# A fused attention and two-MoE kernel: the first token group's x prepared during the last pair of heads, the upper part of decoded weights written by ScalarE, and x items spread over each group

## The chip, the cores and the metric

The kernel runs on one core of a Trainium2 chip. The metric is the device time of one execution in microseconds (us); less is better. The engines of the core run side by side, each with its own instructions in program order: PE (TensorE, the matmuls), ACT (ScalarE), DVE (VectorE), POOL (GpSimd) and SP (SyncE, which here does little but issue DMAs). An instruction waits for semaphores that other engines or DMAs raise, and whatever stands behind it on its own engine waits with it.

## The reference, cut to what matters

```python
def _attn_ref(q, k, v):                       # 4 batches, 8 heads, 1152 positions, 64 per head
    q_pool = q.reshape(B, H, S // 2, 2, D).mean(axis=3)
    scores = np.matmul(q_pool, k.transpose(0, 1, 3, 2)) / np.sqrt(D)
    attn = np.exp(scores - scores.max(-1, keepdims=True))
    return np.matmul(attn / (attn.sum(-1, keepdims=True) + 1e-09), v)

def _moe_ref(x, w_in, w_out):                 # 2304 tokens, 512 -> 2048 -> 512
    h = x @ w_in
    g = np.where(h >= 1, h, np.where(h <= -1, 0.0, (h + 1) ** 2 / 4))
    return g @ w_out                          # then a second MoE: 8 experts, each token to one

reference: x = _moe2_ref(_moe_ref(concat_heads(_attn_ref(q, k, v)), w_in, w_out), ...)
```

The weights of the first MoE are handed in as float64; the kernel decodes them bit by bit.

## The kernel before

**Stages.** Attention runs first, then the dense MoE (called Moe1 here), then the one with experts. All products are done in split precision: a value is kept as an upper part in fp32r (`hi`) and the remainder (`lo = x - hi`), and products of parts are added.

**Attention.** 16 pairs of heads, 9 steps to a pair, 144 steps, numbered s, and 8 steps more to drain. The loop is `Attention.run`, its order is the order of the program. Step s issues the scores of tile s on PE into one PSUM buffer (`scores`), their row minimum and copy `e` on DVE, the transposes of tile s-2 on PE (`probs_t`), their upper part `pth` on ACT and the rest `ptl` on DVE, the exponential of tile s on ACT, and 8 of the matmuls with v (`av`) on PE. Results of `av` are copied to `avs` by ACT and sent to DRAM (`av_b`, `av_t`) by SP; sums of rows go to DRAM as `rs_b`. Raw q, k, v lie in a pool `a_prep`; POOL splits them for the next pair. The last pair is n = 15, steps 135 to 143.

**From attention to Moe1.** The first 640 tokens (group 0 of four) need x in SBUF, transposed. Three pieces of it come from DRAM for each of four row blocks: one part of the sums of products into `xth` and the reciprocals of the sums into `xtl` (`x_raw`, 32 DMAs in all, issued by SP), and the other part into staging tiles `rows` and `row` (`x_load`, 5 DMAs). Five items follow, one for each `parts` entry (`x_item`): two POOL operations (`x = (hi + x) * r`), and later `ev`: `xth` by an ACT copy and `xtl` by a DVE subtraction. Before the change `x_load` is issued at s = 135 (line 1428, in `aside`), the `a_prep` pool is given back at s = 141 and `x_raw` issued there (`tail`, called at line 380), and the items run from s = 144 on, in the drain. In SP's program order `x_load` comes first, then the DMAs of the sums and results of pair 14, then `x_raw`. Raw weights of Moe1 for j = 3 are loaded at s = 147.

**Moe1.** Four groups of tokens, 16 steps j each; step j takes 128 of the 2048 hidden columns. PE does `h` of step j in two halves of 320 tokens, 12 matmuls each (`h_mm`, two PSUM buffers), then the 15 matmuls of `y` of step j-1 (`y_mm`). Between them ACT and DVE make g of h (`h_act`): Relu and Square on ACT, one DVE operation that also sets the PSUM buffer of h free, the upper part `gh` on ACT, the rest `gl` on POOL (group 0) or DVE. During group 0 the weights for j = 3 to 15 are decoded: each has two halves, and each half is three pieces, `first`, `second` and `third`, one DVE operation each; `third` also makes the upper part `wh` and the rest `wl`, both on POOL. A piece is issued at each `fill()`: two in each half of a step and one at its end, five to a step. The x of the next group is made meanwhile: `x_raw` at j = 1, 3, 5, 7, `x_load` from j = 8, the items one after the other from j = 9.

Of the kernel before, what the change touches and what calls it, by code (L numbers as in the profile page):

```python
# [8 lines left out]
F32 = mybir.dt.float32  # L9
# [37 lines left out]
EARLY = 3  # L47
# [27 lines left out]
class Attention:  # L75
# [11 lines left out]
    def open(self, ctx):  # L87
        tc, nc = self.tc, self.nc

        def pool(name, bufs, **kw):  # L90
            return ctx.enter_context(tc.tile_pool(name=name, bufs=bufs, **kw))

        self.prep = tc.alloc_tile_pool(name="a_prep", bufs=1, side="right")
        self.ktp = pool("a_kt", 2)
        self.sp = pool("a_s", 3)
        self.sm = pool("a_sm", 3)
        one = pool("a_one", 1)
        self.ps_s = pool("a_ps_s", 1, space=PSUM)
        self.ps_a = pool("a_ps_a", 1, space=PSUM)
        self.ps_b = pool("a_ps_b", 1, space=PSUM)  # L100
        self.ps_v = pool("a_ps_v", 2, space=PSUM)
        self.pth = one.tile([128, 9, RING], F32R, name="pth")
        self.ptl = one.tile([128, 9, RING], F32R, name="ptl")
        self.vh = one.tile([128, 18, 128], F32R, name="vh")
        self.avs = one.tile([128, 2 * NQ], F32, name="avs")

        self.qts = [one.tile([128, 2, QW], F32R, name=f"qt{i}") for i in range(2)]

        self.bd = [one.tile([128, 2, 128], F32R, name=f"bd{i}") for i in range(2)]
        self.kk = one.tile([128, 2, S], F32R, name="kk")  # L110
        self.r = one.tile([128, 32], F32, name="r")
        self.nc.vector.memset(self.r, 1.0)
# [29 lines left out]
    def load_v(self, n):  # L142
        b, hp = divmod(n, 4)
        d = self.st[n]
        d["vr"] = self.prep.tile([128, 18, 64], F32, name="vr")
        self.nc.sync.dma_start(
            out=d["vr"].rearrange("p (h c) d -> p h c d", h=2),
            in_=self.v[b, 2 * hp:2 * hp + 2].rearrange("h (p c) d -> p h c d", p=128),
        )
# [171 lines left out]
    def run(self, aside, tail):  # L321
# [7 lines left out]
        g = collections.deque()  # L329
# [10 lines left out]
        for s in range(nt + 8):  # L340
# [36 lines left out]
            for _ in range(8 if s < nt else 16):  # L377
                if self.avq:
                    self.avq.popleft()()
            if s == nt - 3:  # L380
                self.prep.release()
                g.extend(tail())
            if self.post and self.post[0][0] < s:
                self.post.popleft()[1]()
            if s >= nt and g:
                for f in g.popleft():
                    f()
            aside(s)
# [8 lines left out]
class Weights:  # L397
# [38 lines left out]
    def decode(self, j):  # L436
# [7 lines left out]
        for i in range(2):  # L444
# [11 lines left out]
            def third(i=i, box=box):  # L456
                nc.vector.scalar_tensor_tensor(out=box["w"], in0=raw[j, i][:, :, 0], scalar=29, in1=box["w"],
                                               op0=ALU.logical_shift_right, op1=ALU.bitwise_or)
                w = box["w"].bitcast(F32)
                hi_part(nc.gpsimd, hi[:, i], w, nc)  # L460
                nc.gpsimd.tensor_sub(out=lo[:, i], in0=w, in1=hi[:, i].bitcast(F32))

            out += [first, second, third]
# [3 lines left out]
class Moe1:  # L467
# [151 lines left out]
    def run(self, route, xt2, moe2):  # L619
# [4 lines left out]
        for k in range(len(steps) + 1):  # L624
            self.flush()
            if k < len(steps):
# [3 lines left out]
                if j == 0 and g + 1 < ng:  # L630
# [12 lines left out]
                            load(i + 2)  # L643
                        return f
                    nxt = [lambda i=i, item=item: item(i) for i in range(m)]
                if g + 1 < ng and j in (1, 3, 5, 7):
                    self.x_raw(g + 1, [slice(j // 2, j // 2 + 1)])
                if g + 1 < ng and j == 8:
                    load(0)
                    load(1)  # L650
                if g + 1 < ng and j == 9:
                    self.xprep.extend(nxt)
                if (g, j) == (2, 10):
                    turn = route.turn(self)
                if (g, j) == (2, 12):
# [716 lines left out]
def tile_kernel(tc, q, k, v, w_in, w_out, emb, tau, w1, w2, out):  # L1372
    nc = tc.nc
    with ExitStack() as ctx:
# [19 lines left out]
        with ExitStack() as actx:  # L1394
# [14 lines left out]
            def aside(s):  # L1409
# [16 lines left out]
                if s == last:  # L1426
                    for i in range(5):
                        m1.x_load(0, i, ws.rows(i, 5))
                if s == last + 12:
                    ws.load(EARLY)  # L1430

            def tail():
# [72 lines left out]
```

## Time and profile before

| what | us |
|---|---|
| runs (3): median, lowest, highest | 1203.81, 1201.74, 1203.91 |
| the profiled execution | 1205.57 |
| its span, first to last instruction | 1203.8 |
| PE busy in the span | 1149.5 (95%) |
| DVE, ACT, POOL busy | 883.3 (73%), 740.3 (61%), 600.7 (50%) |
| TensorE's granted clock, mean | 0.983 |

The span is the time from the first to the last instruction of the profiled execution; 1.8 us more lie around it. Busy shares are means over stages: attention ends at about 481 us, group 0 of Moe1 lasts from there to about 622 us, Moe1 as a whole to about 920 us. A wait is read as the idle time of an engine ahead of an instruction and what ended it. The granted clock is given as a share of full speed, 2.4 GHz; its lower level is 0.5, 1.2 GHz.

### The profile page before, as it was taken

To read this page: it belongs to the slowest core of one execution; us is meant where nothing else is said; L and a number is where in the kernel's file an instruction comes from. 1 tells how busy PE (TensorE), PEld (TensorE's weight loads), DVE (VectorE), ACT (ScalarE), POOL (GpSimd) and SP (SyncE) were. 2 spreads that over 40 slices of the span, in tenths; PEclk is the share of its full clock that TensorE was granted. 3 is DMA by queue.
4 is the path that set the end of the run, shared out by engine and by line. 5 is a ranking of instruction groups with operands and counts; after the bars stand their busy time and mean duration, and the time that the engine had idled before them with its cause. 6 is when DMAs were issued, how large, how long until landed. Compare 5 with 4: busy or idle time off the path is not lost. (4 is left out here: it accounts for less than half of the span.)

```text
span 1203.8 us, 21165 instructions
## 1 busy us (share of the span) xinstructions
PE 1149.5 (95%) x7315; PEld 1068.2 (89%) x7315; DVE 883.3 (73%) x1593; ACT 740.3 (61%) x1451; POOL 600.7 (50%) x523
## 2 busy tenths in 40 slices
PE   7999999999999999799789999999999899999995
PEld 7999999999999999688679889988989798888794
DVE  6888988999999998698745664664444767576663
ACT  5888888878788787343335444444445466576663
POOL 7998988777888883699930230013020311122121
PEclk9999999999999999999899999999999899999998
DMA  7787777785868753564332212111240111376533
GB/s 187 179 184 179 165 186 171 171 209 126 205 162 205 173 137 103 158 194 147 101 106 65 66 45 76 56 34 31 97 159 27 40 51 38 116 256 191 177 106 110
DMA packets 87189, 156.14 MB, mean 130 GB/s; under 512 B 26871, under 2 KB 44279, under 8 KB 87056
## 3 DMA queue, kind: packets, MB, share of 16 engines
q1 hardware_dynamic: 82352, 142.34, 44.2%
q0 software_dynamic: 4336, 11.58, 2.9%
q8 instruction: 67, 1.10, 0.4%
q10 hardware_dynamic: 368, 0.59, 0.2%
q14 instruction: 66, 0.54, 0.2%
HBM read 145.84 MB, written 20.08 MB: 138 GB/s over the span
## 5 line engine op out<-in xcount | busy, mean ns | idle before, releaser
L235 DVE TENSOR_SCALAR_CACHE_REDUCE e<-sc 128x1152 f32<-128x1152 f32 x144 | 194.7, 1352 | 25.0 <-PE sc L231 23.8
L242 ACT ACTIVATE e<-e,nm 128x1152 f32<-128x1152 f32 x144 | 183.7, 1276 | 4.4 <-DVE e L235 4.4
L231 PE MATMUL sc<-kT,qt 128*128 128x384 f32 x780 | 159.8, 340 | 9.2 <-DVE e L235 7.5
L269 ACT CAST pth<-pa 128x768 fp32r<-128x768 f32 (+2 forms) x160 | 116.3, 737 | 83.4 <-PE pa L260 83.4
L271 DVE TENSOR_TENSOR ptl<-pa,pth 128x768 fp32r<-128x768 f32 (+2 forms) x160 | 138.8, 876 | 20.6 <-ACT pth L269 8.4
L1166 DVE TENSOR_TENSOR e<-e,e 128x512 fp32r<-128x512 f32 x200 | 129.4, 686 | 33.0 <-ACT e L1165 16.4
L582 DVE SCALAR_TENSOR_TENSOR u<-h,u 128x320 f32<-128x320 f32 (+1 forms) x112 | 55.7, 497 | 124.8 <-ACT u L581 124.7
L578 ACT ACTIVATE u<-h,half 128x320 f32<-128x320 f32 (+1 forms) x112 | 59.7, 533 | 139.1 <-PE h L563 125.6
L231 PEld LDWEIGHTS sc<-kT,qt 128*128 128x128 f32 x780 | 132.8, 189 | 11.5 <-DVE e L235 9.1
L1255 PE MATMUL d_po<-e,e 128*128 128x512 f32 x504 | 122.6, 396 | 0.5 <-DVE e L1166 0.5
L260 PE MATMUL pa<-idf,e 128*128 128x128 f32 x864 | 118.2, 273 | 1.7 <-DVE ptl L271 1.7
L1165 ACT CAST e<-e 128x512 fp32r<-128x512 f32 x200 | 113.7, 619 | 4.6 <-DMA e<-moe_w 4.1
L595 PE MATMUL y<-wh,gl 128*128 128x512 f32 x288 | 114.0, 396 | 0.5 <-POOL gl L586 0.5
L595 PE MATMUL y<-wh,gh 128*128 128x512 f32 x288 | 114.0, 396 | 0.0
L595 PE MATMUL y<-wl,gh 128*128 128x512 f32 x288 | 113.6, 395 | 0.0
L1263 POOL DMA_INDIRECT out<-d_ob,d_rec x19 | 21.9, 1154 | 181.1 <-ACT d_ob L1262 150.7
L1255 PEld LDWEIGHTS d_po<-e,e 128*128 128x128 f32 x504 | 93.5, 190 | 19.4 <-DVE e L1166 0.9
L260 PEld LDWEIGHTS pa<-idf,e 128*128 128x128 f32 x864 | 103.4, 141 | 7.1 <-DVE ptl L271 1.3
L584 ACT CAST gh<-u 128x320 fp32r<-128x320 f32 (+1 forms) x112 | 52.4, 468 | 87.3 <-DVE u L582 87.3
L563 PE MATMUL h<-xth,wh 128*128 128x320 f32 (+1 forms) x448 | 89.8, 322 | 16.6 <-POOL wh L57 9.8
L285 PE MATMUL av<-pth,vh 128*128 128x288 f32 x576 | 103.5, 307 | 0.0
L535 POOL TENSOR_TENSOR xl<-xth,xl 128x512 f32<-128x512 f32 (+1 forms) x14 | 18.4, 1311 | 168.4 <-DMA xl<-av_t 86.6
(256 smaller groups left out, 2644.6 us busy)
## 6 DMA issues: line engine op xcount, KB each, us to landing
e<-moe_w SPq DMA_DIRECT2D x104, 512.0 KB
kr<-k SPq DMA_DIRECT2D x63, 288.0 KB
qr<-q SPq DMA_DIRECT2D x62, 288.0 KB
kk<-kT SPq DMA_DIRECT2D x60, 288.0 KB
vr<-v SPq DMA_DIRECT2D x16, 576.0 KB
av_b<-avs SPq DMA_DIRECT2D x64, 128.0 KB
wi<-moe_w_in SPq DMA_DIRECT2D x16, 512.0 KB
wo<-moe_w_out SPq DMA_DIRECT2D x16, 512.0 KB
```

What stands on the lines that cost most here:

```text
L231: nc.tensor.matmul(s[:, j, 0:384], lhsT=a, rhs=b[:, 384 * j:384 * j + 384], start=i == 0, stop=i == len(mm) - 1)
L235: nc.vector.tensor_scalar(out=e.rearrange("p (a b) -> p a b", a=3), in0=s[:, :, 0:384], scalar1=-0.5 / D ** 0.5, scalar2=None, op0=ALU.mul ...
L242: self.nc.scalar.activation(e, e, AF.Exp, bias=d["nm"][:, t:t + 1], scale=-1.0, accum_out=d["sum"][:, t:t + 1])
L260: nc.tensor.transpose(p[:, c // 3, (c % 3) * 128:(c % 3) * 128 + 128], e[:, i * 128:(i + 1) * 128], idf)
L269: nc.scalar.copy(hi, p)
L271: nc.vector.tensor_sub(out=lo, in0=p, in1=hi.bitcast(F32))
L285: nc.tensor.matmul(box["t"][:, 0:GQ], lhsT=self.vh[:, h * 9 + i % 9], rhs=p[:, i % 9, c0:c0 + GQ], start=i == 0, stop=i == 17)
L563: nc.tensor.matmul(ps[:, :n], lhsT=a[:, k], rhs=b[:, k, h0:h0 + n], start=i == 0, stop=i == 11)
L595: self.nc.tensor.matmul(y, lhsT=a, rhs=b, start=j == 0 and q == 0, stop=j == NF - 1 and q == 2)
L1165: self.nc.scalar.copy(hi, r)
L1166: self.nc.vector.tensor_sub(out=lo, in0=r, in1=hi.bitcast(F32))
L1255: self.nc.tensor.matmul(self.o, lhsT=(self.hh, self.hl)[a][f // 4][:, f % 4, s], rhs=self.w[b, f // 2][:, f % 2], start=f == 0 and q == 0, ...
```

## The change

Five edits:

- Raw v gets a pool of its own (`a_v`), so that `a_prep` holds q and k alone and can be given back when the last split of q and k is done.
- `a_prep` is given back, and `x_raw` of group 0 issued, at s = 135 instead of 141; the items run from s = 138 instead of 144.
- The raw weights for j = 3 are loaded at s = 146 instead of 147.
- The upper part of weights decoded in group 0 (j >= 3) is made by ACT instead of POOL.
- In every group, `x_raw` is issued at j = 0, 2, 4, 6, the first two `x_load` at j = 1, and the items at j = 3, 5, 8, 10, 12.

```diff
@@ Attention.open
         self.prep = tc.alloc_tile_pool(name="a_prep", bufs=1, side="right")
+        self.vp = pool("a_v", 1)
@@ Attention.load_v
-        d["vr"] = self.prep.tile([128, 18, 64], F32, name="vr")
+        d["vr"] = self.vp.tile([128, 18, 64], F32, name="vr")
@@ Attention.run
-            if s == nt - 3:
+            if s == nt - 9:
                 self.prep.release()
                 g.extend(tail())
             if self.post and self.post[0][0] < s:
                 self.post.popleft()[1]()
-            if s >= nt and g:
+            if s >= nt - 6 and g:
                 for f in g.popleft():
                     f()
             aside(s)
@@ Weights.decode, third
-                hi_part(nc.gpsimd, hi[:, i], w, nc)
+                hi_part(nc.gpsimd if j < EARLY else nc.scalar, hi[:, i], w, nc)
                 nc.gpsimd.tensor_sub(out=lo[:, i], in0=w, in1=hi[:, i].bitcast(F32))
@@ Moe1.run
-                if g + 1 < ng and j in (1, 3, 5, 7):
+                if g + 1 < ng and j in (0, 2, 4, 6):
                     self.x_raw(g + 1, [slice(j // 2, j // 2 + 1)])
-                if g + 1 < ng and j == 8:
+                if g + 1 < ng and j == 1:
                     load(0)
                     load(1)
-                if g + 1 < ng and j == 9:
-                    self.xprep.extend(nxt)
+                if g + 1 < ng and j in (3, 5, 8, 10, 12) and nxt:
+                    self.xprep.append(nxt.pop(0))
@@ tile_kernel, aside
-                if s == last + 12:
+                if s == last + 11:
                     ws.load(EARLY)
```

How the order of instructions moves, at three places.

SP at the head of the last pair of heads (step 135). `kk` and `bd` are the last copies for that pair, `rows` and `row` are `x_load`, `rs_b` the sums of pair 14, `av_b` and `av_t` its results. Before:

```order
L204 DMA kk<-kT 64x1152 x2
L206 DMA bd_123<-qt_121 64x64 x2
L524 DMA rows<-av_b_72 128x512 x4
L524 DMA row<-av_t_76 128x4x128
L309 DMA rs_b_81<-rt 9x32 x4
L317 DMA av_b_75<-avs 64x512
L318 DMA av_t_77<-avs 64x64
```

After the change the 32 DMAs of `x_raw` (`xth` and `xtl`) stand between `bd` and `rows`; these are the last 8 of them and what follows:

```order
L500 DMA xth<-av_b_72 128x512
L508 DMA xtl<-rs_b_78 64x512 x2
L500 DMA xth<-av_t_76 128x128
L508 DMA xtl<-rs_b_78 64x64
L508 DMA xtl<-rs_b_79 64x64
L508 DMA xtl<-rs_b_78 64x64
L508 DMA xtl<-rs_b_79 64x64
L525 DMA rows<-av_b_72 128x512 x4
L525 DMA row<-av_t_76 128x4x128
L310 DMA rs_b_81<-rt 9x32 x4
```

`x_raw` has passed from behind `x_load`, the sums and the results of pair 14 to in front of all of them.

DVE in steps 139 to 141 (before: `e` of the scores, then `ptl` of the tile two steps back):

```order
L235 TENSOR_SCALAR e,nm<-sc 128x1152
L271 TENSOR_TENSOR ptl<-pa,pth 128x6x128
L271 TENSOR_TENSOR ptl<-pb,pth 128x3x128
L235 TENSOR_SCALAR e,nm<-sc 128x1152
L271 TENSOR_TENSOR ptl<-pa,pth 128x6x128
```

After:

```order
L236 TENSOR_SCALAR e,nm<-sc 128x1152
L272 TENSOR_TENSOR ptl<-pa,pth 128x6x128
L272 TENSOR_TENSOR ptl<-pb,pth 128x3x128
L541 TENSOR_TENSOR xtl<-rows,xth 128x512
L236 TENSOR_SCALAR e,nm<-sc 128x1152
L272 TENSOR_TENSOR ptl<-pa,pth 128x6x128
L272 TENSOR_TENSOR ptl<-pb,pth 128x3x128
L541 TENSOR_TENSOR xtl<-rows,xth 128x512
```

The subtraction of each of the five items now stands between two steps of attention, in front of the next `e`; its ACT copy stands in the same way behind the exponential of its step.

ACT in the first steps of group 0 (`u` is Relu from `h` or Square from `u`, `gh` the upper part of g). Before:

```order
L584 CAST gh<-u 128x320
L578 ACTIVATE u<-h,half 128x320
L581 ACTIVATE u<-u 128x320
L584 CAST gh<-u 128x320
L578 ACTIVATE u<-h,half 128x320
L581 ACTIVATE u<-u 128x320
```

After:

```order
L585 CAST gh<-u 128x320
L579 ACTIVATE u<-h,half 128x320
L59 CAST wh_6391<-wf 128x512
L582 ACTIVATE u<-u 128x320
L585 CAST gh<-u 128x320
L579 ACTIVATE u<-h,half 128x320
L59 CAST wh_6391<-wf 128x512
L582 ACTIVATE u<-u 128x320
L585 CAST gh<-u 128x320
L579 ACTIVATE u<-h,half 128x320
L582 ACTIVATE u<-u 128x320
L59 CAST wh_6455<-wf 128x512
```

The copies `wh` have come in from POOL; depending on the fill they stand ahead of Square, ahead of `gh`, or at the end of a step.

## Rows read from the trace of the kernel before

**Rows 1.** Timeline, PE, 460 to 500 us: start, length, engine, line, operation [idle <-releaser].

```profile
460.20 1.21 PE L231 MATMUL sc<-kT,qt 128*128 128x384 f32 x6
...
463.30 1.21 PE L231 MATMUL sc<-kT,qt 128*128 128x384 f32 x6
...
480.79 0.45 PE L563 MATMUL h<-xth,wh 128*128 128x320 f32 x2
...
485.78 0.63 PE L563 MATMUL h<-xth,wh 128*128 128x320 f32 x1 [3.42 <-DMA rs_b<-rt]
...
493.27 0.85 PE L563 MATMUL h<-xth,wh 128*128 128x320 f32 x4 [2.22 <-DVE u L582]
```

**Rows 2.** Timeline, PE, late in group 0; the two longest of its waits.

```profile
585.49 1.43 PE L563 MATMUL h<-xth,wh 128*128 128x320 f32 x4 [3.12 <-POOL wh L57]
...
607.81 0.85 PE L563 MATMUL h<-xth,wh 128*128 128x320 f32 x4 [4.00 <-POOL wh L57]
```

**Rows 3.** Windows: length, busy us of PE, PEld, DVE, ACT, POOL, clock, DMA, GB/s.

```profile
480.80:493.30 12.50, 6.06 (x27) 4.76 (x25) 4.09 (x8) 3.20 (x7) 5.61 (x4) 0.86 0.57 176
500.00:570.00 70.00, 70.00 (x389) 62.59 (x387) 63.66 (x73) 28.92 (x62) 64.26 (x55) 1.00 0.54 169
570.00:613.00 43.00, 32.45 (x151) 27.99 (x150) 30.62 (x33) 13.66 (x28) 38.25 (x32) 0.88 0.32 98
585.50:591.50 6.00, 6.00 (x22) 6.00 (x23) 4.62 (x5) 1.45 (x3) 5.90 (x5) 0.50 0.37 120
607.80:613.00 5.20, 5.19 (x25) 5.19 (x26) 1.09 (x2) 1.46 (x3) 1.31 (x2) 0.67 0.00 0
952.00:956.60 4.60, 4.57 (x16) 3.86 (x17) 1.35 (x2) 1.53 (x3) 0.24 (x1) 0.50 0.31 101
```

**Rows 4.** Timeline, SP's DMA issues, 440 to 500 us.

```profile
446.26 2.01 SPq L524 DMA_DIRECT2D rows<-av_b  x4
...
464.17 0.59 SPq L499 DMA_DIRECT2D xth<-av_b  x1
...
483.83 1.52 SPq L309 DMA_DIRECT2D rs_b<-rt  x4
...
487.93 0.54 SPq L417 DMA_DIRECT2D wi<-moe_w_in  x1
```

**Rows 5.** Timeline, POOL: the first item of group 0.

```profile
467.44 1.28 POOL L535 TENSOR_TENSOR rows<-xth,rows 128x512 f32<-128x512 f32 x1 [4.80 <-DMA xth<-av_b]
469.00 1.30 POOL L536 TENSOR_TENSOR rows<-rows,xtl 128x512 f32<-128x512 f32 x1 [0.28 <-DMA xtl<-rs_b]
```

**Rows 6.** Timeline, ACT, 460 to 480 us.

```profile
461.33 0.40 ACT L288 COPY avs<-av 128x288 f32<-128x288 f32 x1
...
463.17 1.27 ACT L242 ACTIVATE e<-e,nm 128x1152 f32<-128x1152 f32 x1
...
478.85 1.14 ACT L539 CAST xth<-rows 128x512 fp32r<-128x512 f32 x2
```

**Rows 7.** Timeline, DVE, four stretches.

```profile
461.45 1.36 DVE L235 TENSOR_SCALAR_CACHE_REDUCE e<-sc 128x1152 f32<-128x1152 f32 x1 [0.18 <-PE sc L231]
...
479.85 0.21 DVE L306 STREAM_TRANSPOSE rt<-r 128x32 f32<-128x32 f32 x1
480.22 1.29 DVE L540 TENSOR_TENSOR xtl<-rows,xth 128x512 fp32r<-128x512 f32 x2 [0.16 <-DMA xtl<-rs_b]
...
492.39 0.43 DVE L449 TENSOR_SCALAR wf<-wi 128x512 uint32<-128x512 uint32 x1 [3.03 <-DMA wi<-moe_w_in]
...
604.94 1.34 DVE L457 SCALAR_TENSOR_TENSOR wf<-wi,wf 128x512 uint32<-128x512 uint32 x1
```

**Rows 8.** Groups of instructions, 500 to 570 us: count | busy, mean ns | idle before.

```profile
L461 POOL TENSOR_TENSOR wl<-wf,wh 128x512 fp32r<-128x512 f32 x17 | 24.8, 1456 | 1.4
...
L57 POOL TENSOR_SCALAR wh<-wf 128x512 fp32r<-128x512 f32 x16 | 12.1, 758 | 4.3 <-DVE wf L457 4.3
```

**Rows 9.** One line's instructions: duration ns min/median/max.

```profile
L453 DVE SCALAR_TENSOR_TENSOR wf<-wi,wf x16: 680/1118/2669, 262.5 to 602.6; 128x512 uint32<-128x512 uint32 x16
```

## The prediction

> **What bounds the kernel now.** I read the page's first two parts (PE busy for 95% of the span, nearly everywhere), then the waits of PE, its timeline where it waited, and windows of one microsecond for the clock. PE is the bound, so the change can only win back PE's holes, and there are two places with holes that it touches.
>
> The first is the passage into Moe1. Attention ends on PE at 480.79; h of the second step starts at 493.27, and between them PE is idle for 12.50 - 6.06 = 6.44 us [rows 1, 3]. The first cause is SP: `x_raw` is issued from 464.17 to 483.83, 32 DMAs in 19.66 us, and the items trail it [rows 4]. The second is DVE, which waits until 492.39 for raw weights issued at 487.93 while PE's PSUM buffer hangs on the operation behind [rows 1, 4, 7].
>
> The second place is the end of group 0. From 500 to 570 us PE has no hole, with POOL busy for 64.26 and DVE for 63.66 of 70 us; from 570 to 613, where the five items come on top, PE is idle for 43.00 - 32.45 = 10.55 us, nearly all in waits for POOL's `wh` [rows 2, 3]. The clock falls behind two of the holes: 6.0 us at 0.50 and 5.2 us at 0.67 cost another 6.0 x 0.50 + 5.2 x 0.33 = 4.7 us [rows 3].
>
> **The change part by part.**
>
> *Group 0, what goes.* Giving `wh` to ACT takes 12.1 us of POOL's 64.26 in ten steps, and the items no longer come in one lump [rows 3, 8]. ACT is busy for 28.92 of 70 us and has room [rows 3]. All of 10.55 + 4.7 = 15.3 us can go.
>
> *Group 0, what comes.* First, the weights of the last step. Their `third` ends at 606.28, behind one item's subtraction that the change moves away (1.29 / 2 by its usual length, 1.3 with its wait) [rows 7]. Without it: 605.0, and 0.57 for ACT's copy (1.14 / 2) [rows 6], so 605.6; PE could have started at 607.81 - 4.00 = 603.81 [rows 2]. A hole of 1.8 us stays, now behind DVE. Second, a new wait. ACT must wait for DVE's `third` before its copy, and Square, `gh` or the next Relu stand behind that copy; DVE in turn waits for Square. In three steps there are five `third`s: two ahead of Square, where DVE loses the copy and a Square, about 1.05 us each, and one ahead of the first `gh`, where the second half's Relu comes late by about 1.2. That is 3.3 us in three steps. DVE's idle time before is 6.34 of 70 us, 1.9 in three steps [rows 3]. So 0 to 1.4 us in three steps is not covered, the lower end if DVE gets faster beside an emptier POOL (L453 takes 680 ns at best and 1118 at the median [rows 9]); over five such rounds 0 to 7 us. The items' five subtractions come into the same stretch (5 x 0.65 = 3.2 us), and about 2 us of lead that PE's double buffering gives goes off. Bounds 0 to 8.2; I take 3.4, since DVE's idle time is a row and the relief is only a range. With the 1.8 that is 5.2 us.
>
> *The tail of attention.* Here the change adds a wait. SP now issues `x_raw` as soon as `bd` is out, at 446.26, where `rows` stood [rows 4]. Its 19.66 us end at 465.9, and only then come the `x_load` DMAs that the first item needs. A 256-KB load's landing has no row; bounds are 1.5 us and the 4.46 from 487.93 to 492.39 of a 512-KB one [rows 4, 7]. I take 2.2, half of the latter: 468.1. The item takes 1.28 + 1.30 and a hand-off of 0.1 on POOL [rows 5], so its x is there at 470.8. Its ACT copy stands behind the copy of 461.33, so ACT stands from 461.73 to 470.8 with the next `pth` behind it [rows 6]. DVE's subtraction follows at 471.4 to 472.0, and `e` of step 140 behind that, which ran at 461.45 [rows 7]: 10.6 us later. PE has one buffer for scores, so scores of step 141 (463.30 [rows 1]) wait for it: a hole of about 10 us.
>
> The next three steps are longer too. `e` (1.36), the exponential (1.27), the item's copy (0.57), its subtraction (0.65) and then the next `e` are now one loop, since each stands behind the other on ACT or DVE: 3.85 and about 0.2 of hand-offs, 4.05 us, where the step took 463.30 - 460.20 = 3.10 [rows 1, 6, 7]. Three of them: +2.9. One copy of `avs` falls into the loop (0.40 [rows 6]), and PE comes out of its hole at the lower clock (behind a hole of 4.63 us at 952 it ran 4.57 us at 0.50 [rows 3]), of which I let 0.6 reach the loop. Attention ends 10.6 + 2.9 + 0.4 + 0.6 = 14.5 us later, at 495.3. Bounds: 11 (the loop hidden, the load quick) to 17.
>
> *The start of Moe1.* x is ready by then, so h of step 0 runs at once. Raw weights are now bound by the sums: these were ready at 480.06 [rows 7], 0.7 us before attention's end, so 494.6 now; from the issue of sums to that of the weights it is 487.93 - 483.83 = 4.10 us with the same DMAs between [rows 4]; landing 4.46 later: 503.2. PE followed 493.27 - 492.39 = 0.88 behind: 504.0, which is 10.8 us later than before. PE's new hole ahead of it is about 5.2 us, and behind such a hole 4.6 us at half clock cost 2.3, less 0.6 for small holes that were there before. Group 0's even part starts 12.5 us later. The passage as a whole loses, though its first two waits are gone.
>
> *The rest.* Attention's first 15 pairs keep their order. In groups 1 to 3 PE had no such holes, and the items now have two steps or more between load and use: nothing, bounds -0.5 to +1.
>
> *Sum.* +12.5 - 15.3 + 5.2 = +2.4, with the rest at -0.4 for waits inside the loops that I may count twice: +2.0 us. The profiled execution took 1205.57 us (span 1203.8), so 1207.6; the median of the runs lies 1.76 below it, at 1203.81, so **1205.8 us**.
>
> The Trainium skill (SBUF — State Buffer, Who interferes with whom) says that a DVE operation with two SBUF inputs and a POOL operation that reads SBUF hold their shared port by turns, the later one blocking until the other ends, while ACT has ports of its own. The spread of L453, 680 to 2669 ns [rows 9], is what that would look like. By the rule alone, every copy that leaves POOL gives DVE time back, the uncovered 0 to 1.4 us per round would be near 0, and the sum would be about -1.5.
>
> **The rivals.**
>
> *DVE is freed and the tail is shorter* (faster). POOL's 12.1 us less in 70 speed up the pieces so far that the new loop costs nothing, and x lands in time for a tail of +12.5 instead of 14.5: +10.5 - 15.3 + 1.8 = -3.0, 1200.8 us. For it: the 680 ns of L453 [rows 9]. Against it: the items put 5 x 2.7 us back on POOL in the same stretch.
>
> *ACT and DVE bound group 0* (slower). The place is the five `third`s in three steps; it decides once DVE's pieces with the waits for ACT take more than three steps of PE by over 1.2 us. At the upper end, 8.2 + 1.8: +12.5 - 15.3 + 10.0 = +7.2, 1211 us. For it: DVE was busy for 91% with nothing but its own work [rows 3].
>
> *The change does what it says.* SP gets through `x_raw` in time for the items (the tail costs PE nothing), the late weights alone stay of the passage, about 5 us against the 6.44 us and some 1.7 for the clock (0.86 in the mean over 12.50 us [rows 3]) lost there now: -3 - 15.3 + 5.2 = -13, 1191 us. Against it: 32 issues at 0.61 us each are what SP did before [rows 4].
>
> **How the numbers follow.** A measurement of this kernel tells about 0.2%, 2.4 us, from no change. Forecast, 1202 to 1209: 0.45. Freed DVE, 1198 to 1202: 0.22. ACT and DVE bound, 1209 to 1214: 0.25. As it says: 0.08. The likeliest one's own range is 1202 to 1209; for 8 in 10 it reaches from 1198.5 to 1212. Faster (below 1201.4): 0.08 and 0.18 of the second, 0.26. Within: 0.04 of the second and 0.29 of the forecast, 0.33. Slower (above 1206.2): 0.16 and 0.25, 0.41.
>
> **What would show it.** In the trace of the changed kernel: `x_raw` from 446 to 466 us on SP and the `rows` loads behind it; POOL's first item at about 468; ACT idle from 462 to about 471 with POOL's item as the releaser; PE idle for about 10 us at 463, three steps of over 4 us behind it, h of step 0 at about 495 with no wait for x, and a hole of about 5 us ahead of step 1 with DVE as releaser. At the end of group 0, no wait for POOL's `wh`, but holes of 1 to 2 us behind ACT's. I am wrong if the first item starts well before 467, if PE has no hole near 463, or if group 0 after its second step takes over 10 us more than PE's own work.

## The result and the profile after

The changed kernel takes 1214.80 us in the median of 6 runs (1212.08 to 1219.80), the kernel before 1203.86 (6 runs, 1201.74 to 1207.87): a ratio of 1.0092 with a 95% interval of 1.0074 to 1.0110. It is slower by 0.9%, and 2.8 us beyond the upper end of the predicted range. The profiled execution after is the shortest of its six, 1212.08 us (span 1210.1), against 1205.57 (span 1203.8) before.

Lines of the changed kernel stand one behind those of the kernel before from line 95 on. First its PE timeline (start, length, engine, line, operation, [idle before <-releaser]), which answers [rows 1, 2]:

```profile
473.74 2.29 PE L232 MATMUL sc<-kT,qt 128*128 128x384 f32 x6 [11.74 <-DVE e L236]
...
488.37 0.84 PE L261 MATMUL pa<-idf,e 128*128 128x128 f32 x6 [1.92 <-DVE ptl L272]
...
495.70 0.75 PE L564 MATMUL h<-xth,wh 128*128 128x320 f32 x4
...
504.23 1.44 PE L564 MATMUL h<-xth,wh 128*128 128x320 f32 x4 [4.84 <-DVE u L583]
...
509.64 0.40 PE L596 MATMUL y<-wh,gh 128*128 128x512 f32 x1
...
594.57 0.85 PE L564 MATMUL h<-xth,wl 128*128 128x320 f32 x4 [1.75 <-POOL wl L462]
...
611.51 0.86 PE L564 MATMUL h<-xth,wh 128*128 128x320 f32 x4 [2.28 <-ACT wh L59]
...
621.86 0.85 PE L564 MATMUL h<-xth,wh 128*128 128x320 f32 x4 [1.33 <-ACT wh L59]
```

There is a new hole of 11.74 us in the tail of attention, the first h (495.70) waits for no x any more, and a hole of 4.84 us stands ahead of the second h. Late in group 0 the waits for POOL's `wh` are gone, and waits for POOL's `wl` and ACT's `wh` are there in their place.

The queue of SP, the first item on POOL, and ACT and DVE at that hole, which answer [rows 4 to 7]:

```profile
444.78 0.59 SPq L500 DMA_DIRECT2D xth<-av_b  x1
...
465.02 2.01 SPq L525 DMA_DIRECT2D rows<-av_b  x4
...
468.04 1.26 POOL L536 TENSOR_TENSOR rows<-xth,rows 128x512 f32<-128x512 f32 x1 [20.22 <-DMA rows<-av_b]
469.38 1.26 POOL L537 TENSOR_TENSOR rows<-rows,xtl 128x512 f32<-128x512 f32 x1
...
459.87 0.40 ACT L289 COPY avs<-av 128x288 f32<-128x288 f32 x1
470.67 0.62 ACT L540 CAST xth<-rows 128x512 fp32r<-128x512 f32 x1 [10.40 <-POOL rows L537]
...
471.32 1.09 DVE L541 TENSOR_TENSOR xtl<-rows,xth 128x512 fp32r<-128x512 f32 x1 [11.51 <-ACT xth L540]
...
503.35 0.43 DVE L450 TENSOR_SCALAR wf<-wi 128x512 uint32<-128x512 uint32 x1 [8.37 <-DMA wi<-moe_w_in]
```

SP issues `x_raw` from 444.78 on, and the `rows` loads only at 465.02; POOL waits for these, ACT for POOL for 10.40 us, DVE for ACT, and PE for the scores' buffer.

Windows of group 0 (length, busy us of PE, PEld, DVE, ACT, POOL, clock, DMA share, GB/s), against [rows 3]:

```profile
510.00:580.00 70.00, 64.64 (x347) 55.87 (x346) 49.90 (x65) 33.98 (x72) 47.15 (x39) 1.00 0.51 164
...
596.00:600.00 4.00, 4.00 (x16) 3.57 (x15) 3.29 (x5) 2.40 (x5) 3.38 (x3) 0.57 0.37 131
...
613.00:617.00 4.00, 4.00 (x17) 4.00 (x18) 3.49 (x6) 1.51 (x3) 1.09 (x1) 0.57 0.20 70
```

The even part of group 0, where PE was busy for 70 of 70 us, has lost 5.4 us, although POOL is down from 64.26 to 47.15 and DVE from 63.66 to 49.90 (DVE in part because less was done in these 70 us: 65 operations against 73). **No engine is full there.** What has come is in the waits of group 0 (engine, line <- what it waited for: us in total, times, longest), before (498 to 620 us) and after (510 to 632 us):

```profile
ACT u L578 <- PE h L563: 31.2, 12, 7.0
ACT gh L584 <- DVE u L582: 30.7, 30, 3.2
...
PE h L563 <- POOL wh L57: 9.8, 4, 4.0
```

```profile
ACT wh L59 <- DVE wf L458: 45.6, 25, 2.9
POOL wl L462 <- ACT wh L59: 35.1, 17, 3.1
...
ACT gh L585 <- DVE u L583: 12.5, 20, 0.6
...
ACT u L579 <- PE h L564: 7.0, 4, 2.4
...
PE h L564 <- DVE u L583: 5.3, 7, 1.3
...
PE h L564 <- ACT wh L59: 3.6, 2, 2.3
```

Before, ACT waited for PE and, ahead of `gh`, for DVE's `u`. Now it waits most for DVE's `third`: at 25 of the 26 halves of weights, 1.8 us each. PE's waits for DVE's `u`, 5.3 us in seven, all lie in the even part and are what it has lost there. With 1.7 us for POOL's `wl`, PE waits 10.6 us in group 0, as much as before (10.5): the holes have moved, not gone.

Where the time went, by the marks of the two traces (us):

| stretch | before | after | difference | predicted |
|---|---|---|---|---|
| start to the scores of step 139 (`sc<-kk,bd`) on PE | 456.59 | 455.13 | -1.5 | 0 |
| from there to the first h | 24.20 | 40.57 | +16.4 | +14.5 |
| first h to first y | 16.76 | 13.94 | -2.8 | -2.0 |
| group 0: first y to the copy of its y rows | 124.97 | 125.58 | **+0.6** | **-10.1** |
| rest of Moe1, to its last transposes (`xc`) | 285.9 | 285.8 | -0.1 | -0.4 |
| from there to the end | 295.4 | 289.1 | -6.3 | 0 |

The last row is no gain of the change. That stage holds the gathers of the experts' tokens: PE waited 4.63 us for one of them before and ran 4.6 us at half clock behind it, and its longest wait for one after the change was 1.21 us. The runs below, which leave that stage as it is, take between 288.9 and 296.4 us for it. At its start the changed kernel is 12.6 us behind; the medians are 10.9 apart.

### The profile page after: what moved, and what is told of

It is laid out like the page before. It is cut to its first block, busy times and chain, and to the rows that moved or that the text cites. A ratio compares the mean times of both kernels' runs of the same rounds, so it can differ in the third digit from the quotient of the medians.

```text
span 1210.1 us, 21182 instructions
## 1 busy us (share of the span) xinstructions
PE 1145.4 (95%) x7315; PEld 1062.4 (88%) x7315; DVE 877.8 (73%) x1593; ACT 752.3 (62%) x1477; POOL 573.6 (47%) x497
## 5 line engine op out<-in xcount | busy, mean ns | idle before, releaser
L286 PE MATMUL av<-ptl,vh 128*128 128x288 f32 x576 | 102.2, 304 | 0.0
L564 PE MATMUL h<-xth,wh 128*128 128x320 f32 (+1 forms) x448 | 89.0, 321 | 14.0 <-DVE u L583 10.1
```

The lines of the kernel that those rows point to most:

```text
L286: nc.tensor.matmul(box["t"][:, 0:GQ], lhsT=self.vh[:, h * 9 + i % 9], rhs=p[:, i % 9, c0:c0 + GQ], start=i == 0, stop=i == 17)
L564: nc.tensor.matmul(ps[:, :n], lhsT=a[:, k], rhs=b[:, k, h0:h0 + n], start=i == 0, stop=i == 11)
```

## The experiments

Names: "tail" is the x of group 0 prepared in the last pair (with the pool for raw v and the load at s = 146), "copy" the upper part of weights on ACT, "spread" the x items' new places. "Copy later" is an order of my own, shown with its run. Group 0 is first y to the first copy of its y rows. All marks are of one profiled execution; of a kernel run once, the time is that run's too. Each run's kernel has line numbers of its own.

| kernel | first h | first y | group 0 | `xc` | time |
|---|---|---|---|---|---|
| before | 480.79 | 497.55 | 124.97 | 908.4 | 1203.86, median |
| the change | 495.70 | 509.64 | 125.58 | 921.0 | 1214.80, median |
| tail | 495.12 | 508.49 | 124.68 | 919.0 | 1216.81 |
| copy | 478.56 | 496.90 | 129.23 | 912.0 | 1208.47 |
| spread | 480.45 | 498.49 | 125.89 | 910.2 | 1206.88 |
| copy + spread | 479.24 | 497.61 | 124.83 | 908.3 | 1203.76 |
| change, loads first | 486.23 | 500.30 | 126.09 | 912.2 | 1202.76 |
| change, copy later | 496.27 | 509.99 | 119.75 | 915.6 | 1209.98 |
| copy + spread, copy later | 478.64 | 496.47 | 117.42 | 899.7 | 1197.09, median |
| loads first, copy later | 484.60 | 498.42 | 119.99 | 904.2 | 1201.95, median |
| the same, fills at step's end (profiled at 1207.51) | 487.77 | 495.16 | 129.27 | 910.3 | 1202.15, median |
| loads shared out, copy later | 482.56 | 490.40 | 123.64 | 899.9 | 1197.34, median |
| the same, weights ahead of raw loads | 482.40 | 490.25 | 119.97 | 896.0 | **1193.44, median** |

### The parts of the change, one by one

**The tail alone.** Edit: of the change's diff the pool, the steps of the release, of the items and of the weights' load, and nothing in Moe1.

> The kernel before with the early preparation of group 0 alone (pool for v, pool given back and x_raw at step 135, items from step 138, weights at 146); group 0 as before. Marks: the first matmul of y (497.55 us before, 509.64 with the whole change), and group 0's length from there to the first copy of its y rows by ACT (125.0 before, 125.6 with the whole change). Theory (the tail's stall comes from this part and is paid in full, group 0 has a trouble of its own): PE idle for 10 to 12 us near 462, first y at 509 to 510, group 0 at 123 to 126. Rival (the two are one: the late start also spoils group 0's decoding): first y at 509 to 510, but group 0 under 115, since the rest of the change would then be innocent.

```profile
473.15 2.29 PE L232 MATMUL sc<-kT,qt 128*128 128x384 f32 x6 [11.93 <-DVE e L236]
...
503.57 1.44 PE L564 MATMUL h<-xth,wh 128*128 128x320 f32 x4 [4.77 <-DVE u L583]
...
618.45 0.93 PE L564 MATMUL h<-xth,wh 128*128 128x320 f32 x4 [4.03 <-POOL wh L57]
```

PE's timeline has the whole loss: the same two holes as in the change, and in group 0 the old waits for POOL's `wh`. First y comes 10.9 us later than before (at 508.49; 509 to 510 expected), group 0 is as long as before.

**Copy and spread, without the tail.** Edit: the rest of the change's diff.

> The kernel before with ACT's copies of decoded weights and the spread items, without the early preparation of group 0. Theory (ACT's copy behind DVE's third piece makes the two engines wait for each other): first y at 497 to 498, group 0 still 122 to 126 us long, ACT waiting for DVE's third piece for 40 us or more in total, and the whole kernel within 3 us of before. Rival (group 0 was spoilt by the late start): group 0 at 110 to 115, the kernel at 1190 to 1195.

```profile
ACT wh L59 <- DVE wf L457: 44.5, 25, 2.9
```

Group 0 takes 124.83 us, as before, with the ACT waits of the change (the row, of its waits from 498 to 622 us). So it is not the tail's late start that keeps the predicted gain from group 0; copy and spread bring none without it.

**The copy alone, and the spread alone.** Edits:

```diff
-                hi_part(nc.gpsimd, hi[:, i], w, nc)
+                hi_part(nc.gpsimd if j < EARLY else nc.scalar, hi[:, i], w, nc)
```

```diff
-                if g + 1 < ng and j in (1, 3, 5, 7):
+                if g + 1 < ng and j in (0, 2, 4, 6):
...
-                if g + 1 < ng and j == 8:
+                if g + 1 < ng and j == 1:
...
-                if g + 1 < ng and j == 9:
-                    self.xprep.extend(nxt)
+                if g + 1 < ng and j in (3, 5, 8, 10, 12) and nxt:
+                    self.xprep.append(nxt.pop(0))
```

> Only the copy of the decoded upper part (parts 6 and 7 of group 0's weights) moves from POOL to ACT; the x items and the tail of attention stay as before. Theory (the copy stands in ACT's order ahead of the square and behind DVE's OR, so every third of a weight part makes ACT wait and DVE's product u waits for ACT's square): the holes of PE named POOL wh go, holes named ACT wh or DVE u take their place, ACT waits for the thirds 40 to 50 us in some 25 waits, group 0 (first y to the first copy of y rows) stays at 123 to 126 us, and the time is 1201 to 1206 us. Rival (it was the spreading of the x items that brought the waits, the copy on ACT alone frees POOL and with it the holes): group 0 is 112 to 118 us and the time 1190 to 1197 us.

> Only the x items (raw loads, transposed loads and the work on POOL) are spread over each group's steps; the copy stays on POOL and the tail of attention stays as before. Theory (POOL's work in group 0 is as much as before, only its place differs; the x of group 1 used to stand at the steps behind the weights): holes of PE named POOL wh stay, earlier or more of them, group 0 is 124 to 130 us, ACT waits for no third of a weight part for more than 15 us in all, and the time is 1202 to 1209 us. Rival (the holes of before came from the x items standing bunched at step 9): the holes go and group 0 is 112 to 118 us, the time 1190 to 1197 us.

With the copy alone: the window of the even part, a wait of DVE in it, and PE's waits from 570 to 626 us.

```profile
500.00:570.00 70.00, 68.75 (x381) 61.28 (x380) 49.20 (x68) 35.17 (x75) 41.48 (x37) 1.00 0.49 155
...
DVE u L582 <- ACT u L581: 13.7, 12, 1.4
...
PE h L563 <- ACT wh L59: 11.0, 4, 3.4
```

With the spread alone: the window of the even part and PE's largest waits, in it and from 570 to 626 us.

```profile
500.00:570.00 70.00, 66.85 (x361) 58.09 (x360) 62.27 (x70) 27.84 (x59) 65.59 (x56) 1.00 0.48 157
...
PE y L595 <- POOL gl L586: 3.1, 4, 1.3
...
PE h L563 <- POOL wh L57: 7.3, 3, 2.7
```

With the copy alone ACT waits for the thirds 45.6 us in 25 waits. The signs are the theory's, and both rivals fall. The sizes of the copy alone were missed: group 0 is 129.23 us (123 to 126 expected) and the time 1208.47 (1201 to 1206). Neither edit wins anything alone, and they fail in different places. With the copy alone PE keeps 68.75 of 70 us in the even part, although DVE waits 13.7 us for ACT's Square there; but late in group 0 four holes stand behind ACT's `wh`, 11.0 us in all, where four stood behind POOL's before (9.8), although POOL is down to 41.48 of 70 us. So relieving POOL alone does not take the late holes away. With the spread alone the even part already loses 3.15 us, most of it to POOL's `gl`.

### What the copy costs: its work, or its place

**Copy and spread, the copy one fill later.** Edit, beside those two (`settle` runs what was put off; it is also called ahead of the matmuls that read the weights):

```diff
+                def parts():
+                    hi_part(nc.gpsimd if j < EARLY else nc.scalar, hi[:, i], w, nc)
+                    nc.gpsimd.tensor_sub(out=lo[:, i], in0=w, in1=hi[:, i].bitcast(F32))
...
+                    self.late.append((j, i, parts))
...
+            self.ws.settle()
             if self.fillers:
                 self.fillers.popleft()()
```

ACT does the same copies, but one that stood ahead of the Square and behind DVE's `third` now stands behind the Square. POOL's `wl` moves with it, so this tests the place of the two together.

> As the run before (copies on ACT, spread items), but the copy and POOL's subtraction are issued one fill later than the third piece, ahead of the next piece, so that what stands behind the copy on ACT no longer waits for DVE; same operations on the same engines. Theory (the order, not the work, costs group 0 its gain): ACT's waits for the third piece under 10 us in total, group 0 at 111 to 116 us, the kernel at 1191 to 1197. Rival (ACT is too slow or too full for the copies, or raw weights land late): group 0 stays over 120.

Its waits (496 to 615 us) and its window of the even part:

```profile
ACT wh L59 <- DVE wf L462: 18.4, 18, 2.3
```

```profile
500.00:570.00 70.00, 69.82 (x386) 62.39 (x385) 65.84 (x73) 37.32 (x78) 57.92 (x44) 1.00 0.51 161
```

The waits fall from 44.5 to 18.4 us (under 10 expected), PE is busy for 69.82 of 70 us again, and group 0 takes 119.1 us: 5.7 less than with the copy in its old place, though not the 111 to 116 I expected. Late in group 0 PE still waits 4.4 us for ACT's `wh` and 2.6 for POOL's `wl`. Timed in more runs:

> The copy on ACT one fill later and the spread x items, with the tail of attention as before: the same kernel as in the look at 1194.75 us, now timed in rounds. Theory (group 0 is 5 to 6 us shorter and stays so in every run): median 1194 to 1199 us, a ratio of 0.991 to 0.996 to the kernel before. Rival (the one look drew a good gather in the second Moe): 1200 us or more, ratio 0.997 or more.

1197.09 us in the median of 5 runs (1195.46 to 1197.94), ratio 0.9932 (0.9907 to 0.9957). The theory held for the time. Group 0 is 117.42 us in this execution: nearly the same waits of PE as in the 119.1 us of the one before (7.0 us against 7.2), but 1.5 us less of its own time, at a mean granted clock of 1.00 against 0.99. Group 0 of one execution is good to about that.

**The change itself with only this order undone.**

> The changed kernel with one order undone: the upper part's copy on ACT and the rest of a third on POOL are issued one fill later (behind the square and the cast of the activation, not ahead of them); tail, spread and loads as in the changed kernel. Theory (the prediction failed in what the copy's place in ACT's order costs): the tail is as in the changed kernel (hole of 11 to 12 us near 473, first y 508 to 511 us), ACT waits for the thirds 15 to 25 us instead of 45.6, group 0 is 118 to 121 us instead of 125.6, and the time is 1205 to 1210 us. Rival (behind the long tail hole and the late start group 0 is bound by when its weights land and are decoded, so the copy's place is worth little here): group 0 is 124 us or more and the time 1211 us or more.

The tail is as in the change (hole 11.38 us, first y 509.99), ACT waits for the thirds 20.8 us, group 0 takes 119.75 us, and the time is 1209.98. That is 5.8 us of group 0 for the place of the copy and of the `wl` behind it: 3.5 us less of PE's waits, and 2.4 less of its own time (mean granted clock 0.99 against 0.97). The theory held.

PE's idle time in group 0 (us), in the even part of 70 us and in the rest of it, and its busy time, by the windows of each trace:

| kernel | idle, even part | idle, rest | busy |
|---|---|---|---|
| before | 0.00 | 10.55 | 114.42 |
| tail | 0.00 | 10.70 | 113.98 |
| copy | 1.25 | 11.00 | 116.98 |
| spread | 3.15 | 8.30 | 114.44 |
| copy + spread | 4.24 | 7.64 | 112.95 |
| the change | 5.36 | 5.40 | 114.82 |
| copy + spread, copy later | 0.04 | 7.02 | 110.36 |
| change, copy later | 0.63 | 6.66 | 112.46 |

The copy's place costs little in the even part without the spread items, and most of what they cost together goes when the copy moves; 5.4 to 7.6 us late in group 0 stay in either order.

### What the tail costs: work, or SP's queue

**The change with the transposed loads first.** Edit:

```diff
-                if s == last:
-                    for i in range(5):
-                        m1.x_load(0, i, ws.rows(i, 5))
...
+                for i in range(5):
+                    m1.x_load(0, i, ws.rows(i, 5))
                 m1.x_raw(0, [slice(k, k + 1) for k in range(4)])
```

> The whole change with the five x_load DMAs issued ahead of the 32 of x_raw. Theory (the first item waits for x_load, which stands behind x_raw on SP): the items then follow x_raw, which ends at 468 or so instead of 466; item 0 at about 455, the last at about 475; PE's hole near 462 shrinks from 11.7 to under 2 us, the three longer steps stay, attention ends 3 to 6 us later than before instead of 14.9, first y at 498 to 502, group 0 at 124 to 127. Rival (the stall lies in the item's place inside the step, in POOL or in x_raw itself): hole still over 8 us.

```profile
463.26 1.34 PE L232 MATMUL sc<-kT,qt 128*128 128x384 f32 x6 [1.61 <-DVE e L236]
...
494.73 1.44 PE L564 MATMUL h<-xth,wh 128*128 128x320 f32 x4 [4.82 <-DVE u L583]
```

Five DMAs that change places with 32 take the hole from 11.74 to 1.61 us and bring the first y 9.3 us forward. The second hole stays. The time of this single run, 1202.76, is flattered by the last stage, which took the 288.9 us named above.

**Loads first, later items, and the copy later.** Edit, beside those: items from s = 140, their ACT and DVE parts in the drain.

> The three parts of the change with two orders changed: the transposed loads of the first group's x stand ahead of its raw loads on SP's queue, the work on POOL begins some steps later than in the change and ACT's and DVE's parts of it stand in the drain of the last pair, and the upper part's copy and the rest of a third are issued one fill later (behind the square, not ahead of it). Theory (order of the queues, not amount of work, cost the time): attention's last steps have no hole over 2.5 us, the first h of the first Moe stands at 479 to 487 us and the first y at 492 to 500 us, group 0 is 117 to 121 us, and the time is 1186 to 1195 us, under both kernels. Rival (the tail's x work costs PE time wherever it stands, and the deferral's gain is lost when group 0 starts earlier than its weights): first y after 503 us or group 0 over 123 us, and the time 1200 us or more.

1201.95 us (10 runs, 1199.78 to 1204.17), ratio 0.9972 (0.9961 to 0.9984): faster than before, but missed by 7 us, and 4.9 us slower than without any tail. First y and group 0 came as expected; two holes did not. PE, ACT and SP:

```profile
474.95 1.51 PE L261 MATMUL pa<-idf,e 128*128 128x128 f32 x6 [4.28 <-DVE ptl L272]
...
472.58 0.40 ACT L289 COPY avs<-av 128x288 f32<-128x288 f32 x1 [3.93 <-DMA av_b<-avs]
...
468.80 0.48 SPq L318 DMA_DIRECT2D av_b<-avs  x1
```

ACT's copy of `av` waits until the results of pair 14 have been stored, and their store stands behind the 32 `x_raw` DMAs on SP. The queue's cost had only moved on to another customer.

**The first step's fills at its end.** Edit: no `fill()` inside `h_act` for g = j = 0, five behind it.

> The kernel with the loads first and the copy one fill later, and in the first step of the first Moe all five fills (thirds of weight decoding) stand at the step's end instead of among the activation's operations. Theory (the hole of about 5 us ahead of the second h ends with DVE's product u because DVE stands behind the decoding of weights that are still landing): that hole falls from about 5 us to under 2 us, first y comes 2 to 4 us earlier against the first h, group 0 may give back 0 to 2 us of it, and the time is 1 to 4 us under the kernel without this. Rival (the second h waits for the activation's own chain of ACT and DVE): the hole stays over 4 us and the time is within 1 us of that kernel's, or later by the fills' bunching.

```profile
506.56 0.43 DVE L455 TENSOR_SCALAR wf<-wi 128x512 uint32<-128x512 uint32 x1 [6.44 <-DMA wi<-moe_w_in]
```

1202.15 us (10 runs, 1198.41 to 1207.83), ratio to the kernel before 0.9986 (0.9966 to 1.0005); without the edit it was 1201.95. The profiled execution, at 1207.51, is one of the three longest of the ten, so its marks say where it waits, not what the edit costs. Both readings were wrong in part. The hole ahead of the second h did go (1.35 us is left, a step on), but DVE then waits 6.44 us for the raw weights of j = 4 and PE 5.97 for DVE. Their load is issued with a `third`, so the edit itself put it off (to 502.24, from 497.72 without the edit), and in both kernels it stands behind `x_raw` of group 1. The wait only moved on to the next weights.

**Loads shared out.** Edit: first the transposed loads and one slice of `x_raw`, the other three slices each behind a store of pair 14, each item and its ACT and DVE parts behind its slice, and the weights for j = 3 at s = 144.

```diff
+                return [[lambda: raw(0)], [], [], [lambda: raw(1), lambda: one(0)], [],
+                        [lambda: raw(2), lambda: one(1)], [do(0)], [lambda: raw(3), lambda: one(2), do(1)],
+                        [], [lambda: one(3), lambda: one(4), do(2)], [do(3)], [do(4)]]
```

> The copy one fill later, the spread x items, and the tail of attention prepared in the last pair with SP's queue shared out: the transposed loads and the first slice of the raw loads first, the other three slices each behind a store of the attention's output, POOL's items, ACT's and DVE's parts one by one behind their slices, and the weights of part 3 loaded before the last stores. Theory (the 4 us hole near 475 of the kernel with all loads first came from ACT's copy of av waiting for a store that stood behind 32 loads on SP, the 4.7 us hole ahead of the second h from DVE waiting for weights issued at 487.8): the hole near 475 falls under 2 us, the hole ahead of the second h under 2.5 us, first h 478 to 482 us, first y 488 to 492 us, group 0 119 to 122 us, and the time 1190 to 1197 us. Rival (the tail's x work costs PE time wherever its loads stand, or the weights' transfer waits on other things): holes of 6 us or more in all between 460 and 500, first y after 495 us, and the time 1198 us or more.

The passage did what was expected, but for the first h (482.56, 478 to 482 expected): a hole of 1.94 us near 474, 0.38 us ahead of the second h, first y at 490.40, 7.2 us earlier than before. Yet the time is 1197.34 us (7 runs, 1193.88 to 1199.49; ratio 0.9941, 0.9920 to 0.9962), no better than with no tail at all: group 0 took 123.64 us, 6.2 more (119 to 122 expected). SP, DVE and PE show why:

```profile
490.87 0.35 SPq L511 DMA_DIRECT2D xth<-av_b  x1
...
494.17 0.59 SPq L423 DMA_DIRECT2D wi<-moe_w_in  x1
...
498.33 0.43 DVE L455 TENSOR_SCALAR wf<-wi 128x512 uint32<-128x512 uint32 x1 [5.99 <-DMA wi<-moe_w_in]
...
499.94 1.43 PE L576 MATMUL h<-xth,wh 128*128 128x320 f32 x4 [4.12 <-DVE u L596]
```

Because of the spread, `x_raw` of group 1 stands at j = 0, ahead of the weights for j = 4.

**The same with the weights ahead of the raw loads.** Edit:

```diff
-                if g + 1 < ng and j in (0, 2, 4, 6):
-                    self.x_raw(g + 1, [slice(j // 2, j // 2 + 1)])
+                if g + 1 < ng and j in (2, 4, 6, 8):
+                    self.x_raw(g + 1, [slice(j // 2 - 1, j // 2)])
```

> The kernel with shared-out loads, and one thing more: the raw loads of the next group's x stand two steps later in each group, so that at the start of the first Moe the load of weight part 4 stands ahead of them on SP, not behind. Theory (in the kernel with shared-out loads the 6 us that the earlier start won were given back by DVE waiting for that part's weights, issued at 494.17 behind raw loads from 490.87, though the buffer was free from about 488): the hole of 4.12 us at 499.94 falls under 1.5 us, group 0 is 117 to 120.5 us with first y at 489 to 492 us, and the time is 1190 to 1195.5 us. Rival (group 0's end is set by the chain of decoding on DVE, ACT and POOL, whose start the earlier attention does not move): the hole moves to later parts, group 0 stays at 122 us or more and ends at 613 us or later, and the time is 1196 us or more.

```profile
489.19 0.54 SPq L423 DMA_DIRECT2D wi<-moe_w_in  x1
...
495.82 0.86 PE L576 MATMUL h<-xth,wh 128*128 128x320 f32 x4 [0.16 <-DVE u L596]
```

The load comes at 489.19 instead of 494.17, the hole of 4.12 us is down to 0.16, group 0 takes 119.97 us, and the median is **1193.44 us** (4 runs, 1188.63 to 1196.01), ratio 0.9901 (0.9867 to 0.9936). The theory held. This version beats both kernels; it has all three parts of the change, in another order on SP, ACT and POOL. That it also beats copy + spread, copy later, which has no tail, is not shown: the intervals of the two ratios, 0.9867 to 0.9936 and 0.9907 to 0.9957, overlap.

## Why the prediction was wrong

**The tail of attention: right, within 2 us.** SP's queue, the first item (468.04 against "about 468") and ACT's idle time (460.27 to 470.67) came as worked out; attention's end moved by 16.4 us against 14.5, within the bounds of 11 to 17. That the item came to the very time was in part luck: `rows` were issued 0.9 us earlier than worked out and took 3.0 us to the item instead of 2.2. The loops behind took 5.05 and 4.30 us instead of 4.05, and the hole of 1.92 us at 488.37 had no place in the sum. The run with the loads first shows that it is SP's order: the hole went from 11.74 to 1.61 us.

**The start of Moe1: right.** No wait for x, a hole of 4.84 us against 5.2, its end at 504.23 against 504.0. First y came 12.1 us later, against 12.5. That the raw weights are its cause is shown by two runs: with the load issued earlier the hole is 0.38 us (loads shared out), and with DVE's pieces out of the way it goes from there but DVE and PE wait for the next weights (fills at the step's end).

**Group 0, what goes: oversized.** I let all of 15.3 us go, because the late holes named POOL's `wh` and POOL was busy for 64.26 of 70 us. The run with the copy alone shows that this does not follow: POOL is relieved, and four holes of 11.0 us stand where four of 9.8 stood, with ACT's name. With the copy's waits mostly gone, group 0 still takes 117.4 to 120 us, 5 to 7.6 us less than before, and about 7 us of late holes stay. What sets these is open. A rival that no run tried is the order itself: five pieces are issued to a step while the weights of a j have six, so the `third` of the last `wi` half is the last piece of the step ahead of the one that reads it, whoever makes its `wh`.

**Group 0, what comes: the step that failed.** I took 5.2 us, 3.4 for the new waits and the items among them and 1.8 for one hole at the end; the measured net of +0.6 means 15.9 if 15.3 goes, beyond the rival's 10.0 as well. The size of one wait was right. In the change's trace of DVE, ACT, DVE, a `third`, the copy behind it, the Square behind that, and `u`:

```profile
532.91 1.67 DVE L458 SCALAR_TENSOR_TENSOR wf<-wi,wf 128x512 uint32<-128x512 uint32 x1
...
534.62 0.62 ACT L59 CAST wh<-wf 128x512 fp32r<-128x512 f32 x1 [2.81 <-DVE wf L458]
535.14 0.47 ACT L582 ACTIVATE u<-u 128x320 f32<-128x320 f32 x1
...
535.71 0.49 DVE L583 SCALAR_TENSOR_TENSOR u<-h,u 128x320 f32<-128x320 f32 x1 [1.13 <-ACT u L582]
```

DVE stands still for 1.13 us, which I had put at 1.05. What was wrong is the sum. In place of the 3.4 us the even part alone lost 5.36, all of it in PE's waits for DVE's `u`; in place of one late hole of 1.8 there are three of 5.4 in all; and I left out the clock behind the new holes: 4 us at 0.57 behind the one at 594.57, and 4 behind the one at 611.51, 8 x 0.43 = 3.4 us. That is 14.2 of the 15.9; the other 1.7 I cannot place. In the even part, the wait that I charged is not the whole cause: with the copy alone DVE waited 13.7 us for Square and PE lost only 1.25, so DVE's idle time did cover most of it, as I had supposed. What it did not cover came with the spread items in the same stretch: 3.15 us with the spread alone, behind POOL's `gl`, and 4.24 with both, behind DVE's `u`. I had put the items at 3.2 us less 2 of lead from the double buffering, and the 2 came from no row. With the same items and the copy one fill later the loss is 0.04 to 0.63 us. Of the 10.7 us by which group 0 was missed, that order makes 5.8 (125.58 against 119.75 in the change with only it undone); the other 4.9 is what remains, and I put it to the oversized gain. My third sign of being wrong, over 10 us more than PE's own work in group 0, came true: 10.8 us of holes alone.

**The rule on the shared port.** The second operation of a piece took 1271 ns with `wi` in the even part before and 985 in the change, with POOL busy for 47.15 us in place of 64.26. That agrees with what the Trainium skill says (SBUF — State Buffer, Who interferes with whom), that a DVE operation with two SBUF inputs contends with a POOL operation that reads SBUF. POOL's busy time alone does not set it: with the copy later it took 1487 ns, more than before, at 57.92 us of POOL. And it did not help the change: DVE's pieces got shorter, and the time went into waiting for ACT. The -1.5 us that I worked out by the rule alone needed DVE's busy time to be what group 0 waits for.

**Sum and forecast.** At the end of Moe1 the sum should have been +2.0; the marks give +12.6. Of the difference 10.7 comes from group 0, 1.1 from the tail and the start together (+13.6 against +12.5), 0.3 from the rest of Moe1, and -1.5 from ahead of the tail, where the kernel before lost time to a lower clock behind a hole at 266.51 us and the profiled execution after did not (rows at the end). The sign with the largest chance, slower, was right. The range ended too low because the rival "ACT and DVE bound group 0" had the right stage and too small a price.

**What stays open.** What sets the late holes of about 7 us; how much of the 5.8 us is the copy's place and how much that of `wl`; whether the tail gains anything on top of the other two parts; and why the last stage takes between 288.9 and 296.4 us in kernels that leave it alone.

## What to carry to other kernels

Work handed to an idle engine was paid for here by its place in that engine's program order more than by its length: an operation that waits for engine A, put ahead of one that A waits for, makes the two engines wait for each other. Move it behind (here one fill later: 5.8 us). And the engine that a hole names is the one that came last, not always the cause: relieve it alone and see whether the hole goes, before counting the whole gain. For a queue of DMAs, count the issues, and put first the few that someone waits for soonest; three times here someone stood behind a batch of raw loads: the `x_load` DMAs (a hole of 11.74 us), a store (4.28) and weights (4.12).

## What the runs showed of the hardware

The clock did not answer to a hole's length alone. In the change the 4 us from 596 ran at 0.57 behind a hole of 1.75 us, while behind the 1.92 us at 488.37 the clock stayed at 1.00:

```profile
488.00:492.00 4.00, 3.63 (x30) 3.67 (x31) 2.86 (x6) 2.91 (x7) 0.00 (x0) 1.00 0.01 4
```

The same place in attention, where both kernels have the same instructions, shows it too: behind a hole of 1.73 us before (266.51) and of 1.72 us after (266.64), the clock was 0.69 and 1.00.

```profile
266.50:272.00 5.50, 5.49 (x27) 5.40 (x28) 4.08 (x6) 4.06 (x7) 0.67 (x1) 0.69 0.89 203
```

```profile
266.60:272.10 5.50, 5.46 (x40) 5.40 (x41) 5.10 (x7) 4.40 (x8) 0.67 (x1) 1.00 0.89 210
```

So a price per hole taken from one place or one execution can be off by about 1.7 us (4 x 0.43, 5.5 x 0.31) at another.
